# Retention and two MLPs on one core: a carried state of 128 rows by 64 columns on quarters of the array, and one conversion step per bank ahead of the seven-product pairs

## Chip, core and metric

One Trainium2 chip, one of its cores. The metric is device time of one execution in microseconds (us), lower is better. Times are the median of three executions; a profile is of one execution, whose own time is given beside its span.

## What is computed

Three parts in a row: a retention layer over 12 blocks of 64 positions for 2 batches and 8 heads of 64 features, then two MLPs of 512 → 2048 → 512 features on the 1536 tokens. Weights come as float64.

```python
for b in range(nb):
    qb, kb, vb = (q[:, :, sl], k[:, :, sl], v[:, :, sl])
    intra = np.einsum('bhic,bhjc->bhij', qb, kb) * Dmask[None]
    intra = np.einsum('bhij,bhjd->bhid', intra, vb)
    inter = np.einsum('bhid,bhde->bhie', qb * lam_pow[None], kv_state)
    out[:, :, sl] = intra + inter
    kb_dec = kb * rev_pow[None]
    kv_state = lam_block[None, :, None, None] * kv_state + np.einsum('bhsd,bhse->bhde', kb_dec, vb)
...
h = np.maximum(x @ w_in, 0.0);  x = h * h @ w_out          # first MLP
h = x @ w_in;  out = np.maximum(0.01 * h, h) @ w_out       # second MLP
```

## The kernel before

**Retention.** The kernel takes blocks of 128 positions: 12 units (2 batches, 6 blocks each; `c` is the block's number in its batch). The 8 heads stand as 4 pairs `p` of two heads `par`; a transposed tile has 128 partitions, the pair's first head on 0 to 63 and the second on 64 to 127. A turn of the loop over units gives TensorE, in the written order: transposes of k and q of unit i+2 (L294), the state products of unit i (L335, into halves of the array's columns; left out in a batch's last block), the output of unit i (L360 and L362) and the scores of unit i+2 (L311, heads on halves of the array's rows, the two halves into two banks). The output of a head is the sum of a product with the carried state (L360, only where c > 0) and one with the masked scores and v (L362). The state tile `st` has, for each pair, 128 rows by 128 columns with the two heads' 64 by 64 blocks on the diagonal and zeros beside them, so L360 contracts over 128 rows for a head that has 64. VectorE masks the scores (L316), adds up the state (L347) and makes the low part of the output (L69, `xlo`), ScalarE copies the transposes (L298) and makes the high part (L68, `xhi`), GpSimd scales k and q and the old state (L329, L304, L342). Matmuls on plain F32 data take two records each in the trace.

**MLPs.** Products run as three F32R products of high and low parts (L503). Each MLP has 4 stages of 512 hidden features; a stage takes two halves of the first weight (`raw<-in_moe_w_in`) and two of the second (`raw<-in_moe_w_out`), a tile of 1 MB each. `converting` (L98) makes F32R pairs out of the float64 words by a chain of steps, one ScalarE step (L114), then VectorE steps (L115, L116, L118, L121, L122, L125), then the pair (L135, L137); in some stages sums of weight blocks follow (L437 to L442). Two raw buffers exist; the next tile's transfer is written behind L122 of the one before the last. Each bank of 12 matmuls in `first` yields twice, and at each yield `convert` writes one step, so the yields set how many conversion steps stand ahead of a bank's other VectorE work. Stages 1 and 2 of the first MLP (`seven`) run their second product for token tiles 0 and 1 with seven products in place of eight (`second_pair`); the sums that it needs (`activate_for_seven`, L482 to L491, `four_sums`, L447 to L451, and the pairs of L68 and L69 named g1h and g1l) are made while `first` runs for tiles 0 and 1.

**What sets the order.** TensorE keeps the written order throughout, the SP queue in the retention part; elsewhere a scheduler orders each engine's instructions when the kernel is built, and every engine then works in that order.

Lines that the prediction speaks of, beside those above: `dma` L64, `fetch` L90, `state` L323, `output` L351, `first` L505, `second_pair` L620. PSUM has 8 banks, given out in turn.

Of the kernel before, what the change touches and what calls it, by code (L numbers as in the profile page):

```python
# [9 lines left out]
F32 = mybir.dt.float32  # L10
# [9 lines left out]
def tile_retention_then_two_mlps(  # L20
# [43 lines left out]
    def dma(dst, src):  # L64
        return nc.sync.dma_start(dst, src)
# [7 lines left out]
    def source(l, s, n, h):  # L73
        w = ((w1, w2), (w3, w4))[l][n]
        if n == 0:
            return w[:, s * FS + h * CW:s * FS + (h + 1) * CW].rearrange("(k p) f -> p k f", p=P)
        return w[s * FS + h * CW:s * FS + (h + 1) * CW, :].rearrange("(k p) f -> p k f", p=P)

    order = [(0, 0, 0, 0), (0, 0, 0, 1), (0, 0, 1, 0), (0, 0, 1, 1)]
    stages = [(l, s) for l in range(2) for s in range(NS)]  # L80
    for before, stage in zip(stages, stages[1:]):
# [8 lines left out]
    def fetch():  # L90
        if todo:
            key = todo.pop(0)
            r = raw.tile([P, 4 * CW], I64, tag="raw", name="raw")
            k = 4 if key[2] == 0 else 2
            dma(r.rearrange("p (k f) -> p k f", k=k), source(*key))
            fetched.append((key, r))

    def converting():  # L98
# [85 lines left out]
    def retention(ctx_att, att):  # L184
# [132 lines left out]

        st = []
        for e in range(2):
            st.append(att.tile([P, NP, P], F32, name=f"st{e}"))  # L320
            nc.gpsimd.memset(st[e], 0.0)

        def state(n):  # L323
            b, c = units[n]
            if c == NCH - 1:
                return
            kn, vn = nats[n, "k"], nats[n, "v"]
            kd = wk.tile([P, NP, 2, D], F32, tag="kd", name="kd")
            nc.gpsimd.tensor_tensor(  # L329
                out=kd, in0=kn.rearrange("s (a r) d -> s a r d", r=2),  # L330
                in1=kdec.rearrange("s (a r o) -> s a r o", r=2, o=1).to_broadcast([P, NP, 2, D]), op=ALU.mult)
            ps = bank()[:, 0:NP * D].rearrange("p (a e) -> p a e", a=NP)
            for p in range(NP):
                for par in range(2):
                    nc.tensor.matmul(ps[par * D:(par + 1) * D, p, :], kd[:, p, par, :], vn[:, 2 * p + par, :],  # L335
                                     start=True, stop=True)
            old, new = st[c % 2], st[(c + 1) % 2]
            if c:
                tmp = wk.tile([P, NP, D], F32, tag="tmp", name="tmp")
                for par in range(2):  # L340
                    r = slice(par * D, (par + 1) * D)
                    nc.gpsimd.tensor_tensor(out=tmp[r], in0=old[r, :, r],  # L342
                                            in1=LR[r, :, C - 1:C].to_broadcast([D, NP, D]), op=ALU.mult)
            for par in range(2):
                r = slice(par * D, (par + 1) * D)
                if c:
                    nc.vector.tensor_tensor(out=new[r, :, r], in0=ps[r], in1=tmp[r], op=ALU.add)  # L347
                else:
                    nc.vector.tensor_copy(new[r, :, r], ps[r])

        def output(n):  # L351
            b, c = units[n]
            vn = nats[n, "v"]
            ps = bank().rearrange("p (a s) -> p a s", a=NP)
            for p in range(NP):

                rows = [slice(par * D, (par + 1) * D) for par in range(2)]
                if c:
                    for r in rows:
                        nc.tensor.matmul(ps[r, p, :], st[c % 2][:, p, r], qS[n][:, p, :], start=True, stop=False)  # L360
                for par, r in enumerate(rows):
                    nc.tensor.matmul(ps[r, p, :], vn[:, 2 * p + par, :], Pm[n][:, par, p, :], start=c == 0, stop=True)  # L362
            t, o = divmod(b * S + c * C, TT)
            if xhi[t] is None:
                new_x(t)
            split(xhi[t][:, :, o:o + C], xlo[t][:, :, o:o + C], ps)

        n_units = len(units)
        FILL = TT // C
# [135 lines left out]
    def first(l, s, t, ms=range(KF)):  # L505
        for m in ms:
            if m == 0:
                new_g(t, (l, s) == (0, 0))
            ghi, glo = g[t]
            hi, lo = wts[l, s, 0, m // 2]  # L510
            cs = slice(m % 2 * P, (m % 2 + 1) * P)
            ps = bank()
            ops = []
            for kk in range(KD):
                ops += [(hi[:, kk, cs], xhi[t][:, kk]), (hi[:, kk, cs], xlo[t][:, kk]), (lo[:, kk, cs], xhi[t][:, kk])]
            three(ps, ops[:6], True, False)
            yield True
            three(ps, ops[6:], False, True)
            if (l, s) in seven and t < 2:
                activate_for_seven(t, m, ps)  # L520
            else:
                activate(l, ps, plain(), ghi[:, m], glo[:, m])
            if t == 2 and m % 2:
                opened.add((*stages[stages.index((l, s)) + 1], 0, m // 2) if (l, s) != stages[-1] else None)
            yield True


    def first_pair(s):
# [255 lines left out]
```

## Time and profile before

| what | value |
|---|---|
| time, median of 3 runs | 577.12 us (576.59 to 578.66) |
| the profiled execution, its own time | 577.1 us |
| its span, first to last instruction | 575.3 us |
| TensorE busy (matmul) | 566.2 us, 98% |
| VectorE busy | 413.8 us, 72% |
| ScalarE, GpSimd busy | 303.7 us, 103.3 us |
| mean granted TensorE clock | 0.994 of full speed |

Between the span and the execution's time lie 1.8 us. The busy share is over the whole span; which engine is late at a place is read from the rows further below. A record's busy time is longer than the distance to the next record of its engine, because matmuls are pipelined; distances between starts are what a stretch costs.

### The profile page before, as it was taken

The numbers are of one execution on the slowest core, as the hardware profiler recorded it, in microseconds if no ns is written. First come the engines' busy times: TensorE is split into PE (matmuls) and PEld (weight loads), VectorE is DVE, ScalarE is ACT, GpSimd is POOL, SyncE is SP. The second block draws the span as 40 slices with busy tenths as digits, with TensorE's granted clock in tenths as the row PEclk, the third lists the DMA queues.
The fourth block names the chain that finished last, engine by engine and source line by source line (L and its number), as shares of the span: only waits on it lengthen the run. The fifth ranks groups of instructions, "written<-read, shape, count | busy, mean of one in ns | idle before, by whom it ended". The sixth has DMA issues, their size and how long they took to land.

```text
span 575.3 us, 8060 instructions
## 1 busy us (share of the span) xinstructions
PE 566.2 (98%) x3075; PEld 472.8 (82%) x3075; DVE 413.8 (72%) x579; ACT 303.7 (53%) x477; POOL 103.3 (18%) x115
## 2 busy tenths in 40 slices
PE   7999999999999999999999999999999999999997
PEld 6888888888788888888888888888888888888886
DVE  3588999999927599498478999929782996217222
ACT  2344598556757587757448375453562376225110
POOL 3659100000044503433000000000213010210000
PEclk9899999999999999999999999999999999999999
DMA  8998434665498957999513215341529423651432
GB/s 173 235 218 177 142 130 140 221 190 186 171 157 137 161 168 176 214 254 188 174 38 91 81 34 216 129 164 73 110 49 246 108 32 43 78 87 56 164 111 91
DMA packets 79350, 80.75 MB, mean 140 GB/s; under 512 B 40264, under 2 KB 51792, under 8 KB 79312
## 3 DMA queue, kind: packets, MB, share of 16 engines
q1 hardware_dynamic: 61312, 62.15, 35.2%
q0 software_dynamic: 17472, 17.83, 22.9%
q8 instruction: 24, 0.39, 0.3%
q10 hardware_dynamic: 528, 0.26, 0.2%
q14 instruction: 14, 0.11, 0.1%
HBM read 55.05 MB, written 30.42 MB: 149 GB/s over the span
## 4 chain that ended last, share of the span: by engine, by line
PE 79%; DVE 10%; DMA 5%; issue 3%; ACT 2%; POOL 1%; SPq 0%; ACTq 0%; POOLq 0%; DVEq 0%
PE ps L503 72%; DMA raw<-in_moe_w_in 4%; PE ps L294 2%; DMA raw<-in_moe_w_out 2%; DVE hb L118 2%; PE ps L311 1%; DVE rb L122 1%; DVE hb L125 1%; PE ps L362 1%; DVE hb L115 1%; DVE rb L121 1%; PE ps L335 1%; ACT hb L114 1%; PE ps L220 1%; PE ps L360 1%
## 5 line engine op out<-in xcount | busy, mean ns | idle before, releaser
L503 PE MATMUL ps<-xhi,w1h 128*128 128x512 f32 x288 | 112.2, 389 | 0.0
L503 PE MATMUL ps<-xhi,w1l 128*128 128x512 f32 x288 | 112.0, 389 | 0.0
L503 PE MATMUL ps<-xlo,w1h 128*128 128x512 f32 x288 | 112.0, 389 | 0.0
L616 POOL DMA_DIRECT2D spill<-f x48 | 47.1, 1194 | 348.3 <-ACT f L612 348.2
L612 ACT COPY f<-ps 128x512 f32<-128x512 f32 x84 | 48.4, 585 | 69.6 <-PE ps L503 68.8
L503 PEld LDWEIGHTS ps<-xhi,w1l 128*128 128x128 f32 x288 | 54.1, 188 | 11.3
L503 PEld LDWEIGHTS ps<-xlo,w1h 128*128 128x128 f32 x288 | 54.1, 188 | 11.3
L503 PEld LDWEIGHTS ps<-xhi,w1h 128*128 128x128 f32 x288 | 54.0, 188 | 11.3 <-issue 0.2
L474 DVE TENSOR_TENSOR g0l<-f,g0h 128x512 fp32r<-128x512 f32 x52 | 35.1, 687 | 32.5 <-ACT f L470 20.9
L503 PE MATMUL ps<-w2l,g0h 128*128 128x512 f32 (+1 forms) x132 | 50.5, 383 | 0.0
L503 PE MATMUL ps<-w2h,g0l 128*128 128x512 f32 (+1 forms) x132 | 50.5, 383 | 0.0
L503 PE MATMUL ps<-w2h,g0h 128*128 128x512 f32 (+1 forms) x132 | 50.5, 383 | 0.0
L114 ACT ACTIVATE hb<-raw 128x1024 f32<-128x1024 f32 x32 | 36.8, 1149 | 21.5 <-DVE w2l L137 8.3
L137 DVE TENSOR_TENSOR w2l<-hb,w2h 128x1024 fp32r<-128x1024 f32 x16 | 19.5, 1222 | 39.8 <-ACT w2h L135 39.8
L503 PE MATMUL ps<-g0h,w2h 128*128 128x512 f32 x104 | 40.5, 389 | 0.0
L503 PE MATMUL ps<-g0l,w2h 128*128 128x512 f32 x104 | 40.5, 389 | 0.0
L503 PE MATMUL ps<-g0h,w2l 128*128 128x512 f32 x104 | 40.5, 389 | 0.0
L122 DVE SCALAR_TENSOR_TENSOR rb<-raw,rb 128x1024 f32<-128x1024 uint32 x32 | 39.4, 1231 | 0.4
L125 DVE TENSOR_TENSOR hb<-hb,rb 128x1024 f32<-128x1024 f32 x32 | 39.4, 1231 | 0.4
L118 DVE SCALAR_TENSOR_TENSOR hb<-raw,hb 128x1024 uint32<-128x1024 uint32 x32 | 39.1, 1221 | 0.3
L567 DVE TENSOR_TENSOR f<-ps,f 128x512 f32<-128x512 f32 x40 | 26.2, 684 | 9.9 <-PE ps L503 9.9
L716 DVE TENSOR_TENSOR f<-ps,f 128x512 f32<-128x512 f32 (+1 forms) x25 | 16.7, 668 | 22.9 <-PE ps L503 22.8
(143 smaller groups left out, 1155.0 us busy)
## 6 DMA issues: line engine op xcount, KB each, us to landing
raw<-in_moe_w_in SPq DMA_DIRECT2D x16, 1024.0 KB, 5.7
raw<-in_moe_w_out SPq DMA_DIRECT2D x16, 1024.0 KB, 5.1
spill<-f POOLq DMA_DIRECT2D x48, 256.0 KB, 5.5
spill<-f SPq DMA_DIRECT2D x24, 256.0 KB, 2.8
f<-spill SPq DMA_DIRECT2D x24, 256.0 KB, 3.0
k<-in_k SPq DMA_DIRECT2D x12, 256.0 KB, 5.0
q<-in_q SPq DMA_DIRECT2D x12, 256.0 KB, 5.1
v<-in_v SPq DMA_DIRECT2D x12, 256.0 KB, 5.3
```

Source lines behind the costliest of these rows:

```text
L114: nc.scalar.activation(hf, w_hi.bitcast(F32), AF.Abs)
L118: yield ve.scalar_tensor_tensor(out=hb, in0=w_hi, scalar=0xC0000000, in1=hb, op0=ALU.bitwise_and, op1=ALU.bitwise_or)
L122: yield ve.scalar_tensor_tensor(out=rf, in0=w_lo, scalar=2.0 ** -52, in1=rf, op0=ALU.mult, op1=ALU.mult)
L125: yield ve.tensor_tensor(out=hf, in0=hf, in1=rf, op=ALU.add)
L137: yield ve.tensor_tensor(out=lo, in0=hf, in1=hi, op=ALU.subtract)
L294: nc.tensor.transpose(ps[:, p, :], src[:, 2 * p:2 * p + 2, :].rearrange("s h d -> s (h d)"), ident)
L474: nc.vector.tensor_tensor(out=glo, in0=r, in1=ghi, op=ALU.subtract)
L503: nc.tensor.matmul(ps, a, b, start=start and n == 0, stop=stop and n == len(ops) - 1, skip_group_check=again)
L567: ve.tensor_tensor(out=out, in0=ps[h, where], in1=other, op=ALU.add)
L612: nc.scalar.copy(f, src)
L616: nc.gpsimd.dma_start(dst, f, accum_op=ALU.add)
L716: nc.vector.tensor_tensor(out=a, in0=ps, in1=a, op=ALU.add)
```

## The change

The state is kept as 128 rows by 64 columns, the heads of a pair one above the other. A product with it then takes a quarter of the array: the head's half of the rows, and a half of the columns. Pairs with even p go to one bank with their heads on the columns' halves in order, pairs with odd p to a second bank with the halves exchanged, so four heads in a row name four different quarters. All eight products with the state now stand ahead of the eight with the scores. The exchanged halves carry through: the output is split from two banks in two pieces each, and the first MLP's first weight is loaded with rows of odd groups exchanged, in three transfers in place of one. The scaling and the sum of the state are one instruction each in place of two, and the two clearings of the state are gone. In stages 1 and 2 of the first MLP, `first` for token tiles 0 and 1 gives one conversion step per bank in place of two.

```diff
+    half = [slice(e * D, (e + 1) * D) for e in range(2)]
...
-            dma(r.rearrange("p (k f) -> p k f", k=k), source(*key))
+            dst, src = r.rearrange("p (k f) -> p k f", k=k), source(*key)
+            if key[0] or key[2]:
+                dma(dst, src)
+            else:
+                dma(dst[:, 0:k:2], src[:, 0:k:2])
+                for a, b in ((half[0], half[1]), (half[1], half[0])):
+                    dma(dst[a, 1:k:2], src[b, 1:k:2])
...
-            st.append(att.tile([P, NP, P], F32, name=f"st{e}"))
-            nc.gpsimd.memset(st[e], 0.0)
+            st.append(att.tile([P, NP, D], F32, name=f"st{e}"))
...
-                for par in range(2):
-                    r = slice(par * D, (par + 1) * D)
-                    nc.gpsimd.tensor_tensor(out=tmp[r], in0=old[r, :, r],
-                                            in1=LR[r, :, C - 1:C].to_broadcast([D, NP, D]), op=ALU.mult)
-            for par in range(2):
-                r = slice(par * D, (par + 1) * D)
-                if c:
-                    nc.vector.tensor_tensor(out=new[r, :, r], in0=ps[r], in1=tmp[r], op=ALU.add)
-                else:
-                    nc.vector.tensor_copy(new[r, :, r], ps[r])
+                nc.gpsimd.tensor_tensor(out=tmp, in0=old, in1=LR[:, :, C - 1:C].to_broadcast([P, NP, D]), op=ALU.mult)
+                nc.vector.tensor_tensor(out=new, in0=ps, in1=tmp, op=ALU.add)
+            else:
+                nc.vector.tensor_copy(new, ps)
...
-            ps = bank().rearrange("p (a s) -> p a s", a=NP)
-            for p in range(NP):
-
-                rows = [slice(par * D, (par + 1) * D) for par in range(2)]
-                if c:
-                    for r in rows:
-                        nc.tensor.matmul(ps[r, p, :], st[c % 2][:, p, r], qS[n][:, p, :], start=True, stop=False)
-                for par, r in enumerate(rows):
-                    nc.tensor.matmul(ps[r, p, :], vn[:, 2 * p + par, :], Pm[n][:, par, p, :], start=c == 0, stop=True)
+            ps = [bank()[:, 0:2 * C].rearrange("p (a s) -> p a s", a=2) for _ in range(2)]
+            heads = [(p, par ^ p % 2) for p in range(NP) for par in range(2)]
+
+            def place(p, par):
+                return ps[p % 2][half[par ^ p % 2], p // 2, :]
+
+            if c:
+                for p, par in heads:
+                    nc.tensor.matmul(place(p, par), st[c % 2][half[par], p, :], qS[n][half[par], p, :],
+                                     start=p < 2, stop=False, skip_group_check=True)
+            for p, par in heads:
+                nc.tensor.matmul(place(p, par), vn[:, 2 * p + par, :], Pm[n][:, par, p, :],
+                                 start=c == 0, stop=True, skip_group_check=True)
...
-            split(xhi[t][:, :, o:o + C], xlo[t][:, :, o:o + C], ps)
+            for e in range(2):
+                split(xhi[t][:, e::2, o:o + C], xlo[t][:, e::2, o:o + C], ps[e])
...
-            yield True
+            yield (l, s) not in seven or t == 2
```

Lines of the changed kernel are 7 to 9 higher than those before from `converting` to the MLPs' helpers (L294 is L303, L335 is L343, L360 is L364, L362 is L367, L121 is L130, L122 is L131, L125 is L134).

**TensorE, in the loop over units.** One unit with a state, before (the last two rows stand four times in a row, once for each pair p):

```order
L294 MATMUL ps<-ident,k 128x128 x4
L294 MATMUL ps<-ident,q 128x128 x4
L335 MATMUL ps<-v,kd 64x64 x8
L360 MATMUL ps<-qS,st_168 64x128 x2
L362 MATMUL ps<-Pm,v 64x128 x2
```

and with the change:

```order
L303 MATMUL ps<-ident,k 128x128 x4
L303 MATMUL ps<-ident,q 128x128 x4
L343 MATMUL ps<-v,kd 64x64 x8
L364 MATMUL ps<-qS,st_169 64x128 x8
L367 MATMUL ps<-Pm,v 64x128 x8
L320 MATMUL ps<-qT,kT 128x128 x8
```

The products with the state have moved together ahead of those with the scores; before, the two kinds took turns pair by pair in the same split of the array.

**VectorE, in stage 1 of the first MLP, up to the low part g1l that the seven products wait for.** hb, rb and raw are a weight tile under conversion, f, g0l and g1l the activations. Before:

```order
L122 SCALAR_TENSOR_TENSOR rb<-raw,rb 128x1024
L488 TENSOR_TENSOR g0l<-f,g0h 128x512
L125 TENSOR_TENSOR hb<-hb,rb 128x1024
L491 TENSOR_TENSOR f<-f 128x512
L437 TENSOR_TENSOR rb<-hb 128x256
L438 TENSOR_TENSOR rb<-hb 128x256
L439 TENSOR_TENSOR rb<-rb,hb 128x256
L440 TENSOR_TENSOR rb<-hb,rb 128x256
L69 TENSOR_TENSOR g1l<-f,g1h 128x512
```

and with the change:

```order
L125 TENSOR_SCALAR hb<-hb 128x1024
L444 TENSOR_TENSOR rb<-hb 128x256
L495 TENSOR_TENSOR g0l<-f,g0h 128x512
L445 TENSOR_TENSOR rb<-hb 128x256
L446 TENSOR_TENSOR rb<-rb,hb 128x256
L127 SCALAR_TENSOR_TENSOR hb<-raw,hb 128x1024
L498 TENSOR_TENSOR f<-f 128x512
L447 TENSOR_TENSOR rb<-hb,rb 128x256
L69 TENSOR_TENSOR g1l<-f,g1h 128x512
```

From the first weight tile that is converted after the retention part up to this L69, one each of L121, L122 and L125 has moved behind it, to between the sums of stage 2's weights; all else that stood ahead of it still does.

## Rows read from the trace of the kernel before

**Rows 1.** The page: busy time of each engine, and VectorE in 40 slices.
```profile
PE 566.2 (98%) x3075; PEld 472.8 (82%) x3075; DVE 413.8 (72%) x579; ACT 303.7 (53%) x477; POOL 103.3 (18%) x115
...
DVE  3588999999927599498478999929782996217222
```

**Rows 2.** Waits of TensorE's matmul queue, whole span: total us, times, longest.
```profile
PE ps L335 <- POOL qS L304: 2.4, 1, 2.4
...
PE ps L503 <- DVE g1l L69: 0.9, 1, 0.9
```

**Rows 3.** Stretches: length, busy PE PEld DVE ACT POOL, TensorE clock, DMA share, GB/s.
```profile
20.00:40.00 20.00, 19.82 (x305) 17.63 (x302) 14.59 (x25) 8.59 (x15) 12.77 (x14) 1.00 1.08 239
...
130.00:150.00 20.00, 20.00 (x90) 16.57 (x89) 19.70 (x26) 13.60 (x23) 0.00 (x0) 1.00 0.50 173
```

**Rows 4.** TensorE in order of time, one unit: start, busy, line, shapes, count.
```profile
34.81 0.69 PE L335 MATMUL ps<-v,kd 128*64 128x64 f32 x16
35.33 0.39 PE L360 MATMUL ps<-qS,st 128*64 128x128 f32 x4
35.55 0.39 PE L362 MATMUL ps<-Pm,v 128*64 128x128 f32 x4
...
37.18 1.16 PE L311 MATMUL ps<-qT,kT 64*128 64x128 f32 x16
38.27 0.66 PE L294 MATMUL ps<-ident,k 128*128 128x128 f32 x4
```

**Rows 5.** TensorE in order of time, a change of the array's split.
```profile
38.65 0.27 PE L294 MATMUL ps<-ident,k 128*128 128x128 f32 x1
...
38.76 0.60 PE L294 MATMUL ps<-ident,q 128*128 128x128 f32 x4
39.29 0.44 PE L360 MATMUL ps<-qS,st 128*64 128x128 f32 x4
39.56 0.39 PE L362 MATMUL ps<-Pm,v 128*64 128x128 f32 x4
```

**Rows 6.** TensorE's weight loads in order of time, start of the seven products.
```profile
144.88 0.19 PEld L503 LDWEIGHTS ps<-xhi,w1l 128*128 128x128 f32 x1
...
153.27 0.19 PEld L503 LDWEIGHTS ps<-g1h,sw 128*128 128x128 f32 x1
...
154.33 0.19 PEld L503 LDWEIGHTS ps<-g1h,sw 128*128 128x128 f32 x1 [0.41 <-ACT g1h L68]
155.74 0.19 PEld L503 LDWEIGHTS ps<-g1l,sw 128*128 128x128 f32 x1 [1.23 <-DVE g1l L69]
...
157.47 0.19 PEld L503 LDWEIGHTS ps<-g0h,w2h 128*128 128x128 f32 x1
```

**Rows 7.** VectorE in order of time, up to that g1l.
```profile
147.05 0.69 DVE L121 TENSOR_SCALAR rb<-hb 128x1024 uint32<-128x1024 uint32 x1
...
150.06 1.22 DVE L122 SCALAR_TENSOR_TENSOR rb<-raw,rb 128x1024 f32<-128x1024 uint32 x1
151.19 0.69 DVE L488 TENSOR_TENSOR g0l<-f,g0h 128x512 fp32r<-128x512 f32 x1
...
155.00 0.69 DVE L69 TENSOR_TENSOR g1l<-f,g1h 128x512 fp32r<-128x512 f32 x1
```

**Rows 8.** VectorE in order of time, retention part.
```profile
57.91 0.87 DVE L347 TENSOR_TENSOR st<-ps,tmp 64x256 f32<-64x256 f32 x2
58.97 0.69 DVE L69 TENSOR_TENSOR xlo<-ps,xhi 128x512 fp32r<-128x512 f32 x1 [0.19 <-ACT xhi L68]
```

**Rows 9.** The SP queue in order of time: the second tile of the first weight.
```profile
54.29 0.57 SPq L65 DMA_DIRECT2D raw<-in_moe_w_in  x1
```

**Rows 10.** The chain that ended last, in order of time: start, us, what.
```profile
53.87 0.37 SPq L65
54.29 7.10 DMA raw<-in_moe_w_in
61.41 1.18 ACT hb L114
```

## Prediction

> **What bounds the kernel now.** I read the page first: TensorE's matmuls are busy for 566.2 of the span's 575.3 us, VectorE for 413.8, and VectorE's 40 slices show a block of nines in slices 5 to 11, that is some 58 to 158 us, and a 2 behind it [rows 1]. So TensorE carries the time, and one stretch asks for a second look. Next the waits of TensorE's queue [rows 2]: 2.4 us at the first state product, where the queue has hardly begun, and 0.9 us, once, for the g1l of L69. Nothing else above 0.5 us stands there but the queue's start. A microsecond taken out of TensorE's queue therefore comes off the end, unless VectorE, which stands right behind it in that one stretch, turns it into a longer wait.
>
> Two stretches matter. From 20 to 40 us, inside the retention part, TensorE is busy 19.82 of 20.00 us at the full granted clock, VectorE 14.59, while the DMA share is 1.08 [rows 3]. From 130 to 150 us TensorE is full and VectorE at 19.70 of 20.00 [rows 3]; what is late there is conversion work. The time of the profiled execution is 577.1 us, its span and 1.8 us around it; it lies on the median of 577.12, so sums against it need no correction.
>
> **The product with the state.** In a unit the products with the state (L360) and with the scores (L362) take turns, 0.22 us for each group of four records [rows 4]. A group is two rounds of two records that run side by side on two halves of the columns, so a round is 0.11 us. The four L360 groups cost 0.875 us a unit. With quarters the same 16 records go four at a time: four rounds, 0.44 us, if four can run side by side. No row shows four. The nearest is L335, half as many columns a record: its 16 records pass in 0.52 us, from 34.81 to 35.33, a change of split included [rows 4], so the queue can bring 16 records in that time. Bounds are 0.44 and 0.52 us if quarters run together, and no gain if they don't (a rival below). I take 0.45, near the stream's own length, since part of L335's 0.52 is the change of split ahead of it: saved 0.425 us a unit. Ten of the twelve units have c > 0: **4.25 us saved**.
>
> **Changes of the array's split.** The old turns all use one split (128 rows, 64 columns), the same as the state products ahead of them. The new order goes from that to quarters and back: two more changes in the eight units that have both a state product and c > 0, one more in the two that have no state product: 18. The price of one is seen where transposes (128 by 128) give way to L360 [rows 5]: four transposes that start at 38.76, at 0.11 us each (38.65 to 38.76), would let the next start at 39.20, and it starts at 39.29: 0.09 us. The first group after it then takes 0.27 us (39.29 to 39.56) where later ones take 0.22: 0.05 us. Together 0.14 us; 18 of them are **2.6 us lost**. No row shows a change between these two splits, which share the columns' halves; from below the price is nothing, from above it is that into and out of L311: eight groups from 35.33 end at 37.08 and L311 starts at 37.18, 0.10 us, and its eight rounds, 0.88 us, take 1.09 up to the next split [rows 4], 0.2 in all. I take 0.14, the row with loads of 64 columns. The Trainium skill, TensorEngine Tiling (Array Packing), section Tiling Modes, says that a change of mode, unlike a change of tile within a mode, drains the engine; by it the 2.6 us would stand for quarters too. Net of the retention part: 4.25 − 2.6 = **1.65 us**.
>
> **The wait at 154 us.** The seven products' second group waits for g1h and then g1l [rows 6]. From 144.88 to 153.27 there are 37 loads, 0.227 us each. The twelve from 153.27 to 157.47 take 4.20 us in place of 2.72: the stall costs **1.48 us**. The third edit takes one L121, one L122 and one L125 from ahead of that g1l. By their rows that is 0.69 + 1.22 + 1.22 us (L125 has L122's length), less some 0.09 by which each successor starts early [rows 7]: 2.9 us. One more half microsecond leaves this chain because the eleventh unit's xlo now stands ahead of the first late conversion, which waits for a transfer, not behind it. Sum 3.4 us.
>
> Is that enough? Unstalled, TensorE wants g1l by 154.17 (153.27 and four loads); it ends at 155.69 [rows 7]. With 1.65 us saved it is wanted at 152.5 and would end at 155.69 − 3.4 = 152.3, if the chain starts when it did. The chain starts with the transfer of the second half of the first weight: SP issues the last v load at 53.87, when the ninth unit's output has freed a buffer, the tile right behind it at 54.29, it lands at 61.4, and ScalarE's L114 and VectorE follow [rows 9, 10]. That release comes 1.1 us sooner (six units at 0.14 and one at 0.28 us), but the tile now takes two more issues at 0.37 to 0.57 us each [rows 9, 10], some 0.8 us: 0.3 us sooner in all. Wanted at 152.5, there at 152.0: the stall goes, with half a microsecond to spare.
>
> **What I cost at nothing.** The split in two pieces: VectorE's half-size record takes 0.43 us (two in 0.87) against 0.69 for the whole, so xlo costs 0.18 us more a unit and the state's sum 0.43 less [rows 8]; VectorE has a quarter of 20 us free there [rows 3]. GpSimd loses instructions only. The three steps that moved land in the slice with a 2 [rows 1]; the weight tile of stage 2 that they make is wanted only once the seven products and the next first product are through. The extra issues delay the k and q loads queued behind the first tile by about a microsecond with the DMA share over 1 [rows 3]; TensorE now has no wait on them [rows 2]. If that cover is gone, about a microsecond, once.
>
> Sum: 577.1 − 1.65 − 1.48 = **574.0 us**.
>
> **Rivals.**
> 1. *Two row groups can't write one bank together* (slower). The two heads of a pair go to different halves of the rows and the same bank. For it speaks that every row with two row groups at once, L311, gives each its own bank; against it, that the two heads write different partitions. The Trainium skill, TensorEngine Tiling (Array Packing), section Restrictions and Gotchas, has it that different row tiles cannot use the same bank at the same time. What it would do here: heads start in order, the second waits for the first, the second and third share a row half and run together, and so on; eight heads take five steps of two rounds, 1.09 us in place of 0.875. Ten units lose 2.15 us, the 18 changes 2.6, the stall still goes since TensorE comes later: 577.1 + 4.75 − 1.48 = 580.4 us. It decides if the eight products take over 0.76 us a unit (the break-even: 0.875 − 0.26 for the changes + 0.148 for the stall). Chance 0.12.
> 2. *The change of split is free between these two.* Then 4.25 us are saved; g1l is wanted at 149.9 while the chain, its transfer some 2.2 us earlier, ends at 150.1: 0.2 to 0.4 us of stall stay. 577.1 − 4.25 − 1.1 = 571.7 us. For it: both splits use the columns' halves; against it: every change of split that the trace has costs. Chance 0.16.
> 3. *The conversions come late anyway.* VectorE's chain has half a microsecond to spare, and each first-weight tile of the first MLP now lands two issues later, those of stage 2 with stores between their pieces in SP's queue. If three such tiles cost the chain 0.5 us each, or a late k load holds TensorE in the retention part, 1.5 us come back: 575.5 us. For it: VectorE at 19.70 of 20.00 [rows 3]. Chance 0.20.
>
> **How the numbers follow.** The forecast has 0.48, its own range 573.2 to 574.8; what is left, 0.04, is for what I have not thought of. The range for 8 in 10 takes in rivals 2 and 3 and leaves out rival 1: 571.5 to 577.6. A measurement here tells some 0.5% from no change, 2.9 us: faster means under 574.2. The forecast lies just below that line, so I give it two thirds of its chance there: 0.32, with rival 2 0.48; same has the other third, 0.16, rival 3 and part of rival 1, 0.41; slower, over 580.0, most of rival 1 and the rest: 0.11.
>
> **What would show it.** In the retention part L364 as one group of 16 records of 0.44 to 0.52 us a unit, with gaps of about 0.09 us ahead of it and behind it: the distance from the state product's end to the scores' start falls from 1.85 us to some 1.7. Over 0.8 us for L364 is rival 1; no gap is rival 2. TensorE's queue should have no wait on g1l L69; a wait there of over half a microsecond is rival 3, as is one on a k, q or v load. I am wrong if the retention part ends later than before, or if a new wait of TensorE stands behind 160 us.

## Result: slower, and where the time went

| | median | runs | profiled execution | span |
|---|---|---|---|---|
| before | 576.19 us (575.53 to 578.66) | 6 | 577.1 us | 575.3 us |
| after | 583.18 us (581.24 to 587.33) | 6 | 582.62 us | 580.9 us |

The ratio is 1.0125, 95% interval 1.0086 to 1.0164. The prediction, 574.0 us (571.5 to 577.6), was wrong in sign: it had a gain, and the change loses.

The page of after, TensorE's busy time, VectorE in 40 slices and the granted clock [rows 1]:

```profile
PE 566.3 (97%) x3075; PEld 468.9 (81%) x3075; DVE 410.3 (71%) x581; ACT 305.0 (53%) x489; POOL 95.4 (16%) x105
...
DVE  3558899989926599598478999939874896316222
...
PEclk9989999999999998999999999999999999999999
```

TensorE has the same records and the same busy time, in a span 5.6 us longer. The waits of its queue in after [rows 2]:

```profile
PE ps L510 <- ACT g1h L68: 3.2, 1, 3.2
...
PE ps L303 <- DMA k<-in_k: 1.4, 1, 1.4
PE ps L343 <- DMA v<-in_v: 1.1, 2, 0.7
PE ps L510 <- DVE g1l L69: 0.8, 2, 0.6
PE ps L303 <- DMA q<-in_q: 0.8, 2, 0.4
```

Before, no load of k, q or v stood in this list, and the longest wait of a product with a weight was 0.9 us. TensorE in order of time, one unit of the retention part in after [rows 4]:

```profile
48.21 0.69 PE L343 MATMUL ps<-v,kd 128*64 128x64 f32 x16
48.83 0.67 PE L364 MATMUL ps<-qS,st 64*64 64x128 f32 x16
49.42 1.09 PE L367 MATMUL ps<-Pm,v 128*64 128x128 f32 x16
50.45 1.16 PE L320 MATMUL ps<-qT,kT 64*128 64x128 f32 x16
```

From the state product's start to the scores' start it is 2.24 us, against 2.37 before (34.81 to 37.18 in [rows 4]). So a unit is shorter, by 0.13 us. Yet the part ends no sooner. The MLPs' first weight load, in after and (second fence) in before:

```profile
64.10 0.19 PEld L510 LDWEIGHTS ps<-xhi,w1h 128*128 128x128 f32 x1 [0.17 <-PE ps L367]
```

```profile
63.58 0.19 PEld L503 LDWEIGHTS ps<-xhi,w1h 128*128 128x128 f32 x1 [0.17 <-issue]
```

The loss stands at the second of the two places below, and nowhere later. TensorE's weight loads in after, in order of time: the seven products of stage 1 [rows 6], then those of stage 2.

```profile
154.22 0.19 PEld L510 LDWEIGHTS ps<-g1h,sw 128*128 128x128 f32 x1
154.97 0.19 PEld L510 LDWEIGHTS ps<-g1h,sw 128*128 128x128 f32 x1 [0.56 <-ACT g1h L68]
155.70 0.19 PEld L510 LDWEIGHTS ps<-g1l,sw 128*128 128x128 f32 x1 [0.54 <-DVE g1l L69]
...
217.73 0.19 PEld L510 LDWEIGHTS ps<-g1h,sw 128*128 128x128 f32 x1
221.51 0.19 PEld L510 LDWEIGHTS ps<-g1h,sw 128*128 128x128 f32 x1 [3.59 <-ACT g1h L68]
222.60 0.19 PEld L510 LDWEIGHTS ps<-g1l,sw 128*128 128x128 f32 x1 [0.90 <-DVE g1l L69]
```

A stall, here and in the table further down, is the sum of such distances, where they pass half a microsecond, less the usual 0.23 us each: at 154 us 1.0 us (before 1.6), at 217 us 4.4 us (before none). Counting the MLPs' weight loads from their third, number 630 starts at 207.8 us in both kernels, number 700 at 223.7 us before and 229.6 us after, and the last one 5.9 us later too. Those 5.9 us are the stall and 1.5 us of half clock behind it: the granted clock from 205 to 230 us is 0.93.

What g1h waited for shows on three engines. All engines of after in order of time, from 186 to 200 us:

```profile
186.05 1.23 DVE L131 SCALAR_TENSOR_TENSOR rb<-raw,rb 128x1024 f32<-128x1024 uint32 x1
...
187.31 1.70 SPq L65 DMA_DIRECT2D raw<-in_moe_w_in  x3
...
198.62 2.16 ACT L123 ACTIVATE hb<-raw 128x1024 f32<-128x1024 f32 x2 [4.81 <-DMA raw<-in_moe_w_in]
...
199.76 0.69 DVE L124 TENSOR_SCALAR hb<-hb 128x1024 f32<-128x1024 f32 x1 [5.82 <-ACT hb L123]
```

L131 (L122 before) of stage 2's second w2 tile frees a raw tile. The third edit had moved it from 150 us [rows 7] to 186 us. Only behind it is the fourth stage's first w_in tile fetched (the code counts stages from 0, so this one is its stage 3): at 187.31 us in place of 151.35. The same fetch before:

```profile
151.35 0.38 SPq L65 DMA_DIRECT2D raw<-in_moe_w_in  x1
```

ScalarE's first step of that tile, L123, stands in its queue ahead of stage 2's ReLUs and waits 4.81 us there; VectorE idles 5.82 us; all that makes g1h and g1l comes behind. The `x2` of that row is two tiles: the fourth stage's first w_out tile, which ScalarE began at 176.78 us before, comes right behind the other. VectorE does the steps of both from 199.76 us on and stands idle only 0.26 us up to the g1l at 221.86 us. So the late start and the second tile's work both lie ahead of g1l, and no run parts the two.

### The profile page after: what moved, and what is told of

It is laid out like the page before. It is cut to its first block, busy times and chain, and to the rows that moved or that the text cites. A ratio compares the mean times of both kernels' runs of the same rounds, so it can differ in the third digit from the quotient of the medians.

```text
span 580.9 us, 8079 instructions
## 1 busy us (share of the span) xinstructions
PE 566.3 (97%) x3075; PEld 468.9 (81%) x3075; DVE 410.3 (71%) x581; ACT 305.0 (53%) x489; POOL 95.4 (16%) x105
## 4 chain that ended last, share of the span: by engine, by line
PE 71%; DMA 11%; DVE 9%; ACT 4%; issue 3%; SPq 1%; POOL 0%; DVEq 0%; ACTq 0%; POOLq 0%
PE ps L510 65%; DMA raw<-in_moe_w_in 7%; DVE hb L127 2%; DMA q<-in_q 2%; SPq L65 1%; DVE rb L131 1%; DMA v<-in_v 1%; PE ps L367 1%; PE ps L320 1%; PE ps L303 1%; ACT hb L123 1%; DMA raw<-in_moe_w_out 1%; DVE hb L124 1%; PE ps L364 1%; DVE rb L130 1%
## 5 line engine op out<-in xcount | busy, mean ns | idle before, releaser
L510 PEld LDWEIGHTS ps<-xhi,w1h 128*128 128x128 f32 x288 | 54.1, 188 | 11.4 <-PE ps L367 0.2
L123 ACT ACTIVATE hb<-raw 128x1024 f32<-128x1024 f32 x32 | 36.7, 1150 | 29.0 <-DMA raw<-in_moe_w_in 15.2
L131 DVE SCALAR_TENSOR_TENSOR rb<-raw,rb 128x1024 f32<-128x1024 uint32 x32 | 39.1, 1222 | 0.5
L134 DVE TENSOR_TENSOR hb<-hb,rb 128x1024 f32<-128x1024 f32 x32 | 39.1, 1222 | 0.4
L124 DVE TENSOR_SCALAR hb<-hb 128x1024 f32<-128x1024 f32 x32 | 22.8, 712 | 15.9 <-ACT hb L123 15.6
```

What stands on the lines that cost most here:

```text
L123: nc.scalar.activation(hf, w_hi.bitcast(F32), AF.Abs)
L124: yield ve.tensor_scalar(out=hf, in0=hf, scalar1=2.0 ** -15, scalar2=122368.0, op0=ALU.max, op1=ALU.min)
L131: yield ve.scalar_tensor_tensor(out=rf, in0=w_lo, scalar=2.0 ** -52, in1=rf, op0=ALU.mult, op1=ALU.mult)
L134: yield ve.tensor_tensor(out=hf, in0=hf, in1=rf, op=ALU.add)
L510: nc.tensor.matmul(ps, a, b, start=start and n == 0, stop=stop and n == len(ops) - 1, skip_group_check=again)
```

## Experiments

Two theories at first. **A:** the third edit frees a raw tile 36 us late, ScalarE waits for the transfer behind it, and stage 2's seven products come late. **B:** the first weight's three transfers are what is late. A ratio is against runs of the kernel before in the same session. Stalls are from the profiled execution, in us; the last two columns are starts of weight loads, of the MLPs' first and of number 700 in the count above.

| run | median, runs | ratio to before, 95% | stall at 151 to 160 | stall at 214 to 222 | first load | load 700 |
|---|---|---|---|---|---|---|
| before | 576.19 to 577.18 by session | 1 | 1.6 | 0 | 63.58 | 223.7 |
| after | 583.18, 6 | 1.0125 (1.0086 to 1.0164) | 1.0 | 4.4 | 64.10 | 229.6 |
| e1 | 580.31, 4 | 1.0060 (1.0041 to 1.0080) | 2.3 | 0 | 64.50 | 226.9 |
| e2 | 582.20, 4 | 1.0094 (1.0066 to 1.0122) | 0 | 2.9 | 64.40 | 227.2 |
| e3 | 583.65, 4 | 1.0123 (1.0097 to 1.0149) | 1.4 | 5.7 | 62.19 | 229.6 |
| e4 | 581.39, 4 | 1.0077 (1.0055 to 1.0098) | 1.6 | 2.5 | 63.98 | 226.7 |
| e5 | 579.51, 10 | 1.0041 (1.0012 to 1.0070) | 4.9 | 0 | 65.17 | 231.2 |
| e6 | 577.53, 10 | 1.0010 (0.9990 to 1.0031) | 0 | 1.4 | 63.76 | 223.7 |
| e7 | 579.96, 10 | 1.0059 (1.0035 to 1.0083) | 0 | 2.7 | 64.08 | 225.5 |
| e8 | 581.76, 10 | 1.0081 (1.0056 to 1.0105) | 2.4 | 0.9 | 63.15 | 225.0 |
| e9 | 575.89, 11 | 0.9971 (0.9955 to 0.9986) | 0 | 0.5 | 63.70 | 222.7 |
| e10 | 575.19, 10 | 0.9965 (0.9951 to 0.9979) | 0 | 0 | 62.84 | 221.5 |
| e11 | 576.29, 11 | 0.9998 (0.9973 to 1.0022) | 0.5 | 0 | 63.54 | 222.6 |
| e12 | 584.42, 5 | 1.0111 (1.0067 to 1.0155) | 3.0 | 0 | 62.32 | 225.1 |
| e13 | 576.13, 11 | 0.9978 (0.9963 to 0.9992) | 2.0 | 0 | 61.15 | 221.7 |
| e14 | 580.60, 5 | 1.0074 (1.0060 to 1.0089) | 2.4 | 0 | 62.57 | 225.2 |
| e15 | 574.95, 11 | 0.9970 (0.9952 to 0.9988) | 0 | 0 | 61.73 | 220.3 |
| e16 | 575.58, 10 | 0.9982 (0.9970 to 0.9995) | 1.0 | 0 | 62.37 | 221.9 |

### Which edit: e1 to e4

e1 is the change without its third edit, e2 the third edit alone on the kernel before. The edit of e1, which e2 has the other way round:

```diff
-            yield (l, s) not in seven or t == 2
+            yield True
```

> The whole change without its third edit (two conversion steps per bank, as before). Theory A, the third edit holds back the VectorE step that frees a raw buffer and with it the next transfer: the transfer of the fourth stage's weight goes out near 150 us and not at 187, TensorE has no wait over 0.5 us near 222 us, the wait near 155 us is 2 to 4 us, time 578 to 581 us. Theory B, the three transfers of a first-weight tile are what comes late: the wait near 222 us stays at 3 us or more, time 582 to 584 us.

> The kernel before with the third edit alone. Theory A: the wait at 154 us goes (1.5 us), one of 2 to 4 us at the seven products of stage 2 comes (some 220 us), time 577 to 579 us against 576.2 of before. Theory B: no wait near 220 us, time 574.5 to 575 us.

e3 is the change with one transfer for the first weight, e4 the kernel before with three (`dma(dst[:, 0:k:2], ...)` and one for each half of the rows, not exchanged):

> The whole change, but the first weight of the first MLP comes in one transfer per tile; the exchange of its row halves is left out, so the output is not the reference's. Theory A: the wait near 222 us stays at 2 us or more, the retention part ends 1 to 2 us sooner, time 579 to 581 us. Theory B: no wait near 222 us and none on k, q or v loads, time 573.5 to 576 us.

> The kernel before, with each tile of the first MLP's first weight in three transfers (the same places, nothing exchanged). Theory A: no wait near 220 us; the wait at 154 us grows by the later landing of the second tile to 2 to 4 us, time 577 to 579 us. Theory B: a wait of 3 us or more near 220 us and a wait on k loads in the retention part, time 580 to 583 us.

The third edit alone makes the stall at 217 us (e2), and without it there is none (e1). One transfer in place of three doesn't help while the third edit stands (e3). All engines of e2, which has none of the other edits:

```profile
186.67 0.38 SPq L65 DMA_DIRECT2D raw<-in_moe_w_in  x1
...
193.36 1.12 ACT L114 ACTIVATE hb<-raw 128x1024 f32<-128x1024 f32 x1 [1.30 <-DMA raw<-in_moe_w_in]
...
209.56 1.15 ACT L114 ACTIVATE hb<-raw 128x1024 f32<-128x1024 f32 x1 [2.06 <-DMA raw<-in_moe_w_in]
```

ScalarE waits for the tile that was fetched late, and again for the next one, fetched at 202.39 us (200.39 before). So A holds in that the third edit makes the stall; the medians of e2 and e3 lie some 3 us above its ranges. But the late tile need not be the one that ScalarE waits for. In e3 it landed in time, and the wait is for the next one, which went out at 200.45 us, as before. ScalarE in e3:

```profile
191.50 1.15 ACT L117 ACTIVATE hb<-raw 128x1024 f32<-128x1024 f32 x1
...
211.81 1.12 ACT L117 ACTIVATE hb<-raw 128x1024 f32<-128x1024 f32 x1 [6.26 <-DMA raw<-in_moe_w_in]
```

And B is no rival, it is a second cause: e4 loses 0.8% with no other edit, and A had no stall at 217 us there. In e4 ScalarE's first step waits 4.03 us for the fourth stage's second w_in tile, which is issued in three parts from 200.96 us and lands at 211 us; before, one issue at 200.39 us landed at 207.4. All engines of e4, and ScalarE before:

```profile
200.96 1.77 SPq L65 DMA_DIRECT2D raw<-in_moe_w_in  x3
...
211.04 1.13 ACT L120 ACTIVATE hb<-raw 128x1024 f32<-128x1024 f32 x1 [4.03 <-DMA raw<-in_moe_w_in]
```

```profile
207.42 1.12 ACT L114 ACTIVATE hb<-raw 128x1024 f32<-128x1024 f32 x1 [1.64 <-DMA raw<-in_moe_w_in]
```

The same link, one tile later.

### Can the third edit's aim be had without its harm: e5 to e8

e5 is the quarters without the third edit and with one transfer: heads are exchanged in the scaled q and in the state's rows, so the weight needs no exchange. The part on q:

```diff
-                nc.gpsimd.tensor_tensor(out=qS[i], in0=qT[i], in1=LR, op=ALU.mult)
+                nc.gpsimd.tensor_tensor(out=qS[i][:, 0::2], in0=qT[i][:, 0::2], in1=LR[:, 0::2], op=ALU.mult)
+                for e in range(2):
+                    nc.gpsimd.tensor_tensor(out=qS[i][half[1 - e], 1::2], in0=qT[i][half[e], 1::2],
+                                            in1=LR[half[e], 1::2], op=ALU.mult)
```

e6 is the kernel before with one L125 held back, so that VectorE's run ahead of g1l gets shorter while the raw tile is freed as early as it was. e7 is e5 and e6 together, e8 the changed kernel with this in place of its third edit.

```diff
+        if key == (0, 2, 1, 1):
+            while "split" not in opened:
+                yield None
+            tc.keep_in_program_order(ve.tensor_tensor(out=hf, in0=hf, in1=rf, op=ALU.add))
...
+        opened.add("split")
```

> The products with the state on quarters as in the change, but the halves are exchanged in the scaled q (three GpSimd instructions a unit in place of one) and in the state's own rows, so the output has its heads in order and the first weight stays one transfer; two conversion steps per bank as before. Theory A (third edit holds back a raw tile's release) together with B (the split transfers are late for ScalarE): neither is in this kernel, so no gap in the weight loads stands at 217 to 222 us; the MLP's first load comes some 1.4 us sooner than before (62.2, as with one transfer, against 63.6), the gap near 154 us grows by about as much (from 1.5 to some 2.5 to 3 us, since VectorE's chain starts when it did), and the time is 575.5 to 577.0 us against 576.6 before. Rival C (the quarters themselves cost time later, whatever the transfers): over 578 us with a gap behind 160 us.

> The kernel before with two steps per bank; one L125 (of stage 2's second w2 tile) and with it the sums L437 to L440 behind it are held back until the splits of the seven products, while L121 and L122, which frees the raw tile, stay where they were. Theory A: the next transfer goes out near 151 us as before, no gap at 217 to 222 us, and the gap at 154 us (1.5 us) shrinks to 0.5 us or less, since 1.2 and 1.4 us of VectorE's work leave the chain ahead of g1l: 575.2 us (574.5 to 575.8). Rival D (it is the work moved behind g1l, not the transfer, that makes stage 2's g1h late): the gap at 217 to 222 us stands here too, and the time is 580 us or more.

> The quarters with one transfer and the held-back addition together. Theory A with B: retention some 1.4 us shorter and the gap at 154 us about 1 us (wanted sooner by 1.4 us), no gap behind 160 us: 574.0 us (573.0 to 575.2), below both kernels. Rivals C or D: 578 us or more, with a gap at 217 to 222 us.

> The changed kernel with its three transfers, but two steps per bank and the same held-back addition in place of one step. Theory A: no gap at 217 to 222 us from the raw tile; the gap at 155 us (2.3 us with two steps) falls below 1 us: 578.5 us (577.5 to 579.5), of which some 2 us above e5 and e6 are the price of the three transfers. Theory B alone: the late w_in tile of stage 3 holds ScalarE near 205 to 211 us and a gap of over 1 us at 217 to 222 us appears once TensorE comes sooner: 580 us or more. Rival D: over 582 us.

All four missed; e7's numbers are those of rivals C or D. In e6 the stall at 154 us goes as forecast, and TensorE reaches load 630 1.3 us sooner (206.5 us), but load 700 starts at 223.7 us, to the tenth where it started before. ScalarE in e6:

```profile
207.56 1.12 ACT L114 ACTIVATE hb<-raw 128x1024 f32<-128x1024 f32 x1 [2.72 <-DMA raw<-in_moe_w_in]
```

This wait was there before the change, 1.64 us long (L114 at 207.42 us), and it paced stage 2 with nothing to spare: what TensorE won ahead of it, the transfer took back. In e7 the same transfer landed at 209.33 us, and the stall is longer.

What goes with an early or a late landing of this transfer shows on GpSimd. Three stores of 256 KB each that add to what is in memory (`spill<-f`) go out ahead of it. All engines of before, then of e7:

```profile
193.39 3.52 POOL L616 DMA_DIRECT2D spill<-f  x3
...
200.39 0.38 SPq L65 DMA_DIRECT2D raw<-in_moe_w_in  x1
```

```profile
196.11 3.66 POOL L633 DMA_DIRECT2D spill<-f  x3
...
199.63 0.38 SPq L65 DMA_DIRECT2D raw<-in_moe_w_in  x1
```

Where the stores' issue ended 3.5 us ahead of the tile's, the tile took 7.0 us (before) and 6.5 us (e5), 1.2 us ahead 7.2 us (e2), 0.8 us ahead 8.1 us (e6); where the two met, 9.7 us (e7) and 11.4 us (e3). So in e6 the tile goes out 0.9 us sooner than before and lands no sooner. No run moved the stores: this is read from the traces and not tested.

e5's profiled execution is its slowest (584.26 of 576.62 to 584.26 us): there ScalarE waited 2.9 us for a w_in tile at 128.7 us and the stall at 154 us grew to 4.9 us. The wait on a first weight tile has a third place, in the retention part, in e6 again:

```profile
30.72 1.14 ACT L114 ACTIVATE hb<-raw 128x1024 f32<-128x1024 f32 x1 [3.23 <-DMA raw<-in_moe_w_in]
31.75 0.58 ACT L304 COPY kT<-ps 128x512 f32<-128x512 f32 x1
```

kT's copy, which TensorE's scores need, stands behind it. From this came theory **F**: weight transfers pace TensorE through ScalarE's first conversion step, which stands in order ahead of work that TensorE waits for.

### The link itself: e9 to e12

e9 is e6, with that step of the fourth stage's second w_in tile kept behind the ScalarE work written ahead of it. e10 adds the very first tile, `(0, 0, 0, 0)`. e11 is e10 on e5's quarters. e12 is the changed kernel, third edit and all, with both w_in tiles of the fourth stage so kept.

```diff
-        nc.scalar.activation(hf, w_hi.bitcast(F32), AF.Abs)
+        start = nc.scalar.activation(hf, w_hi.bitcast(F32), AF.Abs)
+        if key in ((0, 3, 0, 1),):
+            tc.keep_in_program_order(start)
...
```

> The kernel before with the held-back addition, and with ScalarE's first step (L114) of the fourth stage's second w_in tile kept behind the work written ahead of it, so that it stands behind stage 2's ReLUs and not among them. Theory F (a weight transfer paces TensorE through that L114: it stands ahead of work that TensorE waits for, in order, until its transfer has landed near 207 us): the gaps at 216 to 219 us, 1.8 us, go, and the microsecond and more that was won at 154 us stays: weight load 700 at 222.4 in place of 223.7, 575.7 us where before has 577.0. Rival G (stage 2's ReLUs and VectorE's work are late by themselves, the L114 only fills the time): the gaps stay and the time is that of before, 577 us.

> As the run before, and ScalarE's first step of the very first w_in tile is kept in its written place too, behind the fifth unit's copies, where it stood ahead of them and waited for a transfer that lands at about 31 us. Theory F: TensorE's wait on the q copies in the retention part (1.5 us, and the half clock behind it) goes or shrinks below 0.5 us, the MLP's first weight load comes 1 to 1.5 us sooner (62.4), of which the gap at 154 us takes back about half: 575.0 us (574.2 to 576.0). Rival H (the k, q and v loads bound this stretch anyway): TensorE waits for loads instead, the first weight load stays at 63.5 or later, and the time is that of the run before.

> The same three changes of order on the version with quarters and one transfer. Theory F: first weight load at 61.5, gap at 154 us of about 1 us, none behind 160 us: 574.2 us (573 to 575.5). Rival H: the retention part ends where it did, near 63.5 to 64, and the quarters are worth nothing: 575.5 to 577 us.

> The changed kernel, one step per bank and three transfers, with ScalarE's first step (there L123) of both w_in tiles of the fourth stage kept behind the work written ahead of it. The raw tile is still freed late, near 186 us, and the transfer still lands near 199 us or later. Theory F: nobody who feeds TensorE waits for it any longer, the gaps at 217.7 and 221.5 us (4.4 us of stall) go, and the time falls from 583.2 to 577.5 us (576.5 to 579). Rival D (it is VectorE's work moved behind g1l that is late): the gaps stay, 582 us or more. If later tiles come late instead, a gap stands behind 240 us.

e9 and e10 came out close to what F had (e9 has the work that e6 moved behind g1l and keeps 0.5 us of stall, so that work is not what makes it, against rival D). In e10 part of the room went to loads, as rival H had it: TensorE waits 1.7 us for v, q and k. e10 is 0.35% under before, the fastest here of the kernels that do the whole work (e3, e13 and e15 leave out the exchange of the weight's rows), and so under after too. In e12 the raw tile is still fetched late (188.74 us), yet the stall at 217 us is gone: a late fetch makes no stall there once nothing that TensorE needs stands behind the tile's first step. That TensorE comes 1.4 us later there (load 630 at 209.2 us) accounts for 1.4 of the 4.4 us at most. e9 and e12 don't part ScalarE's wait from VectorE's work, because VectorE's steps on the tile move back with ScalarE's: in e12 VectorE is busy 18.39 us from 205 to 230 us, in after 24.66. e12's time did not fall, against F's 577.5 us, because the conversions put off came late at the next place, as its last sentence allowed. Weight loads in e12:

```profile
249.61 0.19 PEld L512 LDWEIGHTS ps<-g0l,w2h 128*128 128x128 f32 x1 [2.15 <-DVE g0l L483]
251.95 0.29 PEld L512 LDWEIGHTS ps<-g0l,w2h 128*128 128x128 f32 x1 [1.78 <-DVE g0l L483]
```

e11's quarters gained nothing over e10; time and first load are rival H's numbers and not F's, but loads are not what held it: its trace has a new wait of 1.2 us on the state's sum, at the retention part's end, and three GpSimd instructions a unit in place of one. So the worth of the quarters was still open.

### What the quarters save: e13 to e16

e13 is e10 with the change's own quarters and one transfer (the exchange left out), e14 the same with the three transfers, e15 and e16 are e13 and e11 with the second w_in tile fetched a unit sooner: `if i in (1, 8)` for `(1, 9)`.

> Quarters as in the change with the first weight in one transfer (the exchange of its rows is left out, so the MLPs multiply other rows; the time of the work is the same), two steps per bank, and the three changes of order of e10. Theory I (the saving is real and only masked): the MLP's first weight load at 61.5 us (62.8 in e10 less 1.3), a gap of up to 1 us comes back at 154 us, none behind: 574.2 us (573.5 to 575.0), where e10 has 575.2. Theory H (loads pace the retention part up to 35 us): TensorE waits there for k, q or v by as much as it saved, first load at 62.3 us or later: 575.0 us or more.

> The changed kernel (quarters, three transfers) with two steps per bank and the three changes of order of e10. If the three transfers cost by delaying the k, q and v loads behind the first tile and by landing late at 54 us: waits on k, q and v of 2 us or more in the retention part, first weight load at 62.8 to 63.6 us, gaps at 154 us of some 1.5 to 2.5 us, none behind 160 us: 577 us (576 to 578), some 2 to 3 us above e13. If the transfers cost nothing once the order is mended: within 0.7 us of e13.

> e13 with the second w_in tile's transfer written in the ninth turn of the unit loop in place of the tenth, ahead of the last v load (the exchange of the weight's rows is left out as in e13). Theory K (VectorE's run ahead of g1l starts with that tile): the tile is issued some 2 us or more sooner, the gap at 151 to 153 us (1.97 us of stall in e13) falls below 0.8 us, the time from 576.1 to 574.6 us. Rival L (VectorE and ScalarE are full from there on for other reasons, or the tile delays the last v load): the gap stays within 0.5 us of e13's and so does the time.

> e11 with the second w_in tile's transfer one unit sooner. Theory K: no gap at 154 us; the first weight load stays near 63.5 us unless e11's wait on the state's sum at the end of the retention part goes; 575.5 us. Rival L: 576.3 us as e11.

First weight load in e10, e13 and e15, in this order:

```profile
62.84 0.19 PEld L511 LDWEIGHTS ps<-xhi,w1h 128*128 128x128 f32 x1 [0.17 <-issue]
```

```profile
61.15 0.19 PEld L512 LDWEIGHTS ps<-xhi,w1h 128*128 128x128 f32 x1 [0.17 <-PE ps L369]
...
152.96 0.19 PEld L512 LDWEIGHTS ps<-g1h,sw 128*128 128x128 f32 x1 [1.50 <-ACT g1h L68]
```

```profile
61.73 0.19 PEld L512 LDWEIGHTS ps<-xhi,w1h 128*128 128x128 f32 x1 [0.17 <-PE ps L369]
```

Quarters end the retention part 1.7 us sooner in e13 (62.84 to 61.15), where the forecast had 1.65, and 1.1 us sooner in e15; each is one execution, and the closeness of the first is in part luck. In e13 all of it is lost at 152 us, where the next two groups of loads wait for ScalarE and VectorE, and load 700 stands where it stood in e10. So the saving is real, as theory I had it, and its loss complete, which theory I had not. With the tile fetched sooner (at 49.43 in place of 52.38 us) that stall goes (e15), and load 700 is 1.2 us ahead of e10's: theory K. e16 has its time but kept a stall of 1.0 us. The medians of e15 and e10, from two sessions, don't differ by more than their intervals, so no run shows the quarters' saving in the time of the whole kernel. Three transfers cost 1.4 us of the retention part and 3.4 us by load 700 (e14 against e13, 4.5 us in the medians), half as much again as e14's expectation had. Of the 3.4 us, 0.5 are a longer stall at 154 us and 1.5 the half clock behind it, which e13 has not.

## Why the prediction was wrong, step by step

The profiled span is 8.7 us longer than the forecast had it: 2.2 us of that stand in the retention part, 0.9 at 154 us and 5.9 at 217 us, less 0.3 behind.

- **The product with the state, and changes of split: right.** Saved per unit 0.425 − 0.28 = 0.145 us were forecast, 0.13 measured; quarters do run four at a time (16 records and a change of split in 0.59 us), so rival 1 is refuted, and the changes cost, so rival 2 is. The Trainium skill's rule, by which the 2.6 us would stand (TensorEngine Tiling (Array Packing), Tiling Modes: a change of mode drains the engine), agrees with 0.62 us for the state product ahead of quarters against 0.52 before. The Trainium skill's rule on row tiles and banks (TensorEngine Tiling (Array Packing), Restrictions and Gotchas: different row tiles can't use one bank at the same time) does not show here: both row halves write each bank, in different partitions, in those 0.59 us, where rival 1 had 1.09.
- **"If that cover is gone, about a microsecond, once": mis-sized.** The two extra issues made TensorE wait 3.3 us for k, q and v (1.4, 0.8, 1.1), and then run at half clock from 34.98 to 38.75 us. The wait has two sources: loads that go out later, and a TensorE that came sooner, since in after its clock was full from 10 to 20 us, where it was 0.66 before. At one clock there, 0.83, the three transfers cost 1.4 us (waits on k, q and v of 1.8 us in e14, 0.4 in e13), so the retention part's price was nearly right. What the term left out comes behind: e4, which has the three transfers alone, is 0.8% slower, and e1, the change without its third edit, 0.6%, so this step failed too. The window from 20 to 40 us, of after [rows 3]:

```profile
20.00:40.00 20.00, 17.55 (x265) 14.33 (x258) 9.81 (x20) 7.46 (x16) 9.53 (x10) 0.91 1.14 222
```

  TensorE was "busy 19.82 of 20.00" there in an execution in which it came late; in e6, whose retention part is that of before, its clock from 10 to 20 us is full, and it is busy 18.46 of 20.00. The loads stood close behind. I read a full engine as the only bound.
- **The wait at 154 us: right cause, start mis-sized.** Three steps left the run ahead of g1l, but it began with a tile that landed 2.1 us later, not 0.3 us sooner (ScalarE's L123 starts at 63.55 us where L114 started at 61.41 [rows 10]). The stall fell from 1.6 to 1.0 us only. The third edit does take it away where the tile is not late (e2: none), and without that edit it is 2.3 us (e1).
- **"What I cost at nothing … The three steps that moved land in the slice with a 2": this step failed.** They land at 185 to 188 us, behind the slice with the 2 (158 to 173 us). I followed the converted weight to its reader and not the raw tile to its next transfer, though L122 and the transfer behind it were named in the description of the kernel. A step that frees a buffer has two successors; the second cost 5.9 us in the profile of after, and the third edit as a whole 0.65% by the ratios of after and e1, some 3.7 us. Rival 3 had the right kind (conversions late, one transfer late) at a quarter of the price.
- **574.0 us was out of reach even without the harm.** No kernel here has it: the forecast is a ratio of 0.9946, the lowest measured is 0.9965 (e10). e6 removes the stall at 154 us and is 0.1% from before: the next bound, the transfer at 207 us, had no slack. The wait stood in the trace of before, on ScalarE, with 1.64 us; I had looked at TensorE's waits alone, and an engine that arrives just in time shows none.
- **The signs named.** "I am wrong if the retention part ends later than before, or if a new wait of TensorE stands behind 160 us" — both happened (64.10 against 63.58 us, and 217.73 us).

Open: why TensorE's clock differs between 10 and 20 us from one execution to the next (0.66, 0.83 or 1.00), how the stall at 217 us divides between ScalarE's wait and VectorE's work on two tiles, and whether keeping the stores away from the transfer near 200 us would help. A third raw tile, which would cut the link in another way, was not tried.

## What to carry to other kernels

Before a step is moved, list what it frees as well as what it makes, and follow the freed buffer through the next transfer to the first instruction that waits for it, in order, on its engine. Before a saving is counted to the end, look for the next place where another engine waits for a transfer without TensorE showing it: there the saving can end. An instruction that waits for a far-off transfer belongs behind the work of its engine that TensorE needs now (e9, e10), unless what it puts off is late at the next place (e12).

## What was not expected of the hardware

- A stall can cost more than its gap. Behind the waits at 32.66 to 34.98 us L364's 16 records took 1.07 us to the next start and L367's 1.90, in place of 0.59 and 1.03, at the lower of the clock's two levels, 1.2 GHz (the granted clock is 0.55 from 34.98 to 38.75 us), and 1.5 of the 5.9 us at 217 us are of this kind. It is not so behind every stall: the distances of the weight loads behind it go from 0.23 to 0.43 us in e1 (2.3 us of stall) and e14 (2.4 us), and stay at 0.23 us in e8 (2.4 us), e4 (2.5 us) and e7 (2.7 us). TensorE in after:

```profile
32.66 0.63 PE L303 MATMUL ps<-ident,k 128*128 128x128 f32 x4 [1.39 <-DMA k<-in_k]
...
34.98 0.88 PE L343 MATMUL ps<-v,kd 128*64 128x64 f32 x16 [0.66 <-DMA v<-in_v]
35.78 1.13 PE L364 MATMUL ps<-qS,st 64*64 64x128 f32 x16
36.85 1.97 PE L367 MATMUL ps<-Pm,v 128*64 128x128 f32 x16
```

- One megabyte in three transfers (of 0.5 and twice 0.25) was slower to land than in one: each of the six w_in tiles from 84 to 212 us took 7.1 to 10.1 us from the first issue in e4, 5.4 to 7.0 us before. Part of it is the issuing, whose third part goes out 1.1 to 3.3 us behind the first. For the last of the six the stores of GpSimd count for as much: over the runs it took 6.5 to 11.4 us in one transfer and 6.8 to 10.1 us in three.
